# A top-32 attention with an MLP behind it: loads, MLP steps and the drain in another order

## The chip, the cores and the metric

One Trainium2 chip, one of its cores. The metric is the device time of one execution in microseconds (us), lower is better. Before the change three executions took 823.51, 825.10 and 825.77 us, median 825.10. An execution of the same kernel with the profiler on took 824.92 us.

## The reference

Inputs are q, k, v of shape (8 batches, 8 heads, 576 rows, 64), and an MLP with `w_in` (512 x 2048), `w_out` (2048 x 512) and `alpha` (2048). Per batch and head:

```
scores = (q @ k.T) / sqrt(64)                        # 576 x 576
kth    = the 32nd largest of each row
scores = where(scores >= kth, scores, -1e9)
attn   = exp(scores - max) / (sum + 1e-9)
o      = attn @ v                                    # 576 x 64
x      = o of all heads side by side                 # 4608 x 512
h      = x @ w_in                                    # 4608 x 2048
out    = (max(h, 0) + alpha * min(h, 0)) @ w_out     # 4608 x 512, float32
```

## The kernel before

**Duos.** The attention is cut into 144 duos of two 128 x 576 blocks of scores each, 18 a batch (lines 77 to 91; the drain's `D` is the last, 143). A pair p is two heads that share the 128 partitions. A normal duo `("n", p, j)` is rows 128j to 128j+127 of both heads; since 576 = 4 x 128 + 64, the last 64 rows of four pairs are packed into two "tails" duos `("m", ...)` a batch: duos 8, 9, 26, 27, 44, 45, 62, 63, 80, 81, 98, 99, 116, 117, 130 and 131. In the first six batches the order is j = 0 and 1, tails, j = 2 and 3.

**What a duo needs.** TensorE (PE) makes the scores in a PSUM tile of which there is one (`st_qk`, line 238; 6 matmul records for a normal duo, 16 for tails). ScalarE (ACT) copies them out (`st_exit`, 260). VectorE (DVE) finds a lower bound of the 32nd largest with MAX8 instructions (`dve_slot`, 317, and `threshold_steps`, 289); ACT counts what lies under it with Sign and an accumulator (`st_count`, 372); GpSimd (POOL) multiplies scores and signs (`st_y`, 384); DVE picks the exact value out of that (`row`, `pick_steps`). ACT then makes a large number of all that lies under the threshold with Relu, POOL subtracts it (`st_relu`, 391: two ACT and two POOL instructions), ACT takes Exp into the bf16 tile `w` (`st_exp`, 399), and a DMA transposes `w` into `wT` (`st_wT`, 404; three buffers). PE multiplies by v with a column of ones that gives the sum (`st_av`, 410), DVE divides (`norm_a`, `norm_b`) into the tile `x`, and a DMA transposes that into `xT` (`st_xT`, 467).

**The MLP.** Behind an `xT` stands a chunk of rows (`mlp_ready`, 494). A chunk has `unit`s (16 matmul records of 128 columns or 8 of 256 into one of two PSUM buffers `ph`, then one Relu into `gT`, `h_relu`, 564) and `part`s (five matmuls of 512 columns into `pz`, `o_pe`, 573), and at the end one ACT copy (`o_act`) and a store (`o_sp`). The prelu is folded into a second, linear weight, `w_lin`.

**The order.** It is written out by hand. The main loop (724 to 779) has a slot n for each duo, and within a slot each engine gets: on PE one `h_pe` or a filler (`keep_warm`, four matmuls on zeros), a transpose of q or k, the scores of duo n+1, `st_av` of an older duo, one `o_pe`, and at the end of the slot a second `o_pe` where enough is ready (765). `late` (742) adds one more `h_pe` in an even slot where many units wait. Loads of q, k and v are issued by SyncE (SP) in the middle of the slot (`run(n, "ld")`, 749), the two `xT` transposes of four pairs at its end (777 to 779). Every helper records its instructions in this order for its engine, and each engine, SP's DMA queue among them, works in it: an instruction that waits holds up all behind it.

**The drain.** What is left after slot 143 is a list of calls (808 to 890). There the last four duos but the first, 140 to 143, don't go through Relu and POOL: ACT takes Exp of all scores (`st_all`) and DVE masks them (`st_mask`, two instructions a duo). `T["spare"]` is the scores' PSUM, free by then. At the end `check_low` (678) looks whether any threshold came out invalid; if so a general path computes all again, which the drawn inputs don't need. The program ends when the last store has landed and the engines have met.

Of the kernel before, what the change touches and what calls it, by code (L numbers as in the profile page):

```python
# [12 lines left out]
ALU = mybir.AluOpType  # L13
# [46 lines left out]
def fast_path(tc, q, k, v, moe_w_in, moe_w_out, moe_alpha, out, flag):  # L60
# [32 lines left out]
    with ExitStack() as ctx:  # L93
# [171 lines left out]
        def norm_of(n):  # L265

            return stage.get(("norm", n), 0)

        def pick_steps(m):

            def eq_():
                sm(DVE.tensor_tensor(eq, io9.unsqueeze(1).to_broadcast([128, 4, 9]),
                                     T.pop(("cs", m)).unsqueeze(2).to_broadcast([128, 4, 9]), ALU.is_equal),
                   [(292, 301)], [(256, 292)])

            def pk_():
                pk = T["pk"] = two.tile([128, 4, 9], FP32, name="pk", tag="pk")
                sm(DVE.scalar_tensor_tensor(out=pk, in0=eq, scalar=BIG if m < ND // 2 - 2 else 1.0, in1=T.pop(("p9", m)), op0=ALU.mult,
                                            op1=ALU.mult), [(256, 292), f"p9{m % 3}"], ["pk"])
# [37 lines left out]
        def dve_slot(n, f_late):  # L317
# [19 lines left out]
            if n % 2:  # L337
                fold, negate, least, turn = threshold_steps(n // 2)
                fold()
                h_relu()  # L340
                negate()
            else:
                h_relu()
# [55 lines left out]
        def st_exp(n):  # L399
            w = ws[n % 4]  # L400
            ACT.activation(w[:, :, 0:S], T.pop(("s", n)), AF.Exp, scale=att_scale)
            st_wT(n)

        def st_wT(n):
# [89 lines left out]
        def mlp_ready(xt, rows):  # L494
# [229 lines left out]
        for n in range(ND):  # L724
# [26 lines left out]
            if ready() > 4 or not wide_copy:  # L751
                o_act()
# [36 lines left out]
        def st_mask(d):  # L789
            w, e, s_ = ws[d % 4], T.pop(("e", d)), T.pop(("s", d))  # L790
            for i in range(2):
                r = 2 * d + i
                DVE.scalar_tensor_tensor(out=w[:, i, 0:S], in0=s_[:, i, :], scalar=KT[:, r:r + 1],
                                         in1=e[:, i, :], op0=ALU.is_ge, op1=ALU.mult)
            st_wT(d)

        def normed(d):
            norm_a(d)
# [12 lines left out]
        o_sp()  # L811
        st_av(D - 6)
        h_pe(2)
        h_pe(2)
        h_relu(ACT)
        o_act()
        o_sp()
        st_count(D - 1)
        st_y(D - 1)
        h_relu()  # L820
        picked(D // 2 - 1)
        normed(D - 6)
        st_exp(D - 4)
        st_all(D - 3)
        row(D - 1, 0)
        row(D - 1, 1)
        st_count(D)
        st_y(D)
        st_all(D - 2)
        now[0] += 1  # L830
        fill(1)
        st_av(D - 5)
        fill(1)
        h_pe(2)
        fill(2)
        h_pe(2)
        st_av(D - 4)
        st_mask(D - 3)
        row(D, 0)
        row(D, 1)  # L840
        picked(D // 2)
        normed(D - 4)
        st_mask(D - 2)
        h_relu(ACT)
        st_all(D - 1)
        st_all(D)
        st_mask(D - 1)
        st_mask(D)
        o_act()
        o_sp()  # L850
        h_relu(ACT)
        h_pe(2)
        fill(1)
        st_av(D - 3)
        h_relu(ACT)
        h_pe(2)
        fill(1)
        st_av(D - 2)
        normed(D - 2)
        h_relu(ACT)  # L860
        o_act()
        o_sp()
        now[0] += 2
        h_pe(2)
        fill(1)
        st_av(D - 1)
        h_relu()
        h_pe(2)
        fill(1)
        st_av(D)  # L870
        normed(D)
        h_relu(ACT)
        o_act()
        o_sp()
        turn = 0
        while hq or act or soon or oq or stores:
            now[0] += 1
            while h_pe(2):
                pass
            o_pe()  # L880
            h_relu((DVE, ACT)[turn % 2])
            turn += 1
            if turn == 5:
# [288 lines left out]
```

## Time and profile before

| what | value |
|---|---|
| median of 3 executions | 825.10 us |
| profiled execution, its own time | 824.92 us |
| profiled execution, span of its instructions | 823.1 us |
| span of core 0, mean granted TensorE clock | 0.985 |
| first and last copy of scores out of PSUM | 9.42 and 769.94 us |
| last copy of a result out of PSUM starts | 815.22 us |

The span runs from the first to the last instruction; what lies around it is 1.8 us. Times in the rows are us from the span's start. In the rows of a time line the first number is the start, the second the time taken, and brackets at the end hold how long the engine sat idle before it and what ended that; "x4" behind a shape counts instructions that follow one another and were merged. PEld is TensorE's weight load. Every instruction of the fast path has line 32, the recording helper's, so rows are told apart by the tiles: `s_sb<-ps_sc` is the copy of scores, `sg` the Sign, `r` the Relu, `w` the Exp or the mask, `ph` a unit, `pz` or `spare<-w_out_b` a part, `rest` the filler, `tps` a transpose of q or k on PE, `xo` or `spare<-v,wT` is `st_av`.

### The profile page before, as it was taken

What the parts mean: (1) busy time and instruction counts of PE and PEld (TensorE: products, weight loads), DVE (VectorE), ACT (ScalarE), POOL (GpSimd) and SP (SyncE); (2) the same over time, 40 slices, a digit from 0 to 9 for tenths busy, and PEclk for the clock granted to TensorE, in tenths of its full rate; (3) what the DMA queues carried; (4) which work ended last, traced back from release to release, by engine and by line L of the source; (5) the groups of instructions that cost most, each with busy time, mean ns of one, the idle gap of its engine ahead of it and who ended that gap; (6) DMA issues with size and microseconds to landing.
All of it is one profiled execution on the core that took longest, in us unless ns stands there. A gap on an engine that the chain in (4) does not pass through costs nothing.

```text
span 823.1 us, 17793 instructions
## 1 busy us (share of the span) xinstructions
PE 734.9 (89%) x5351; PEld 424.2 (52%) x5426; DVE 757.5 (92%) x3471; ACT 763.3 (93%) x1257; POOL 745.5 (91%) x701
## 2 busy tenths in 40 slices
PE   8888899989999997988989898897989899999875
PEld 5334455555555554545555555454555555556553
DVE  4999999999999999998999999999899999999941
ACT  5999999999999999998999999999999999999921
POOL 2999999999998999999999999999999998999910
PEclk9999999999999999999999999999999999999989
DMA  7799996556564666665755556656566475544441
GB/s 157 174 192 189 155 170 115 104 119 120 127 134 105 120 126 131 116 123 106 133 109 118 118 113 134 122 128 113 110 130 136 97 122 107 97 98 87 83 85 50
DMA packets 343562, 100.25 MB, mean 122 GB/s; under 512 B 337425, under 2 KB 337441, under 8 KB 343457
## 3 DMA queue, kind: packets, MB, share of 16 engines
q1 hardware_dynamic: 340384, 91.90, 57.2%
q0 software_dynamic: 1872, 6.82, 3.6%
q8 instruction: 45, 0.74, 0.4%
q14 instruction: 61, 0.49, 0.2%
q10 hardware_dynamic: 1200, 0.30, 0.2%
HBM read 36.71 MB, written 9.44 MB: 56 GB/s over the span
## 4 chain that ended last, share of the span: by engine, by line
DVE 46%; PE 17%; ACT 17%; POOL 10%; issue 6%; DMA 3%; SPq 0%; DVEq 0%; ACTq 0%; POOLq 0%
DVE small L32 14%; DVE p L32 11%; DVE up L32 8%; DVE gT L32 5%; PE ps_sc L32 5%; POOL y L32 5%; POOL s_sb L32 5%; ACT r L32 5%; ACT sg L32 4%; PE pz L32 4%; ACT s_sb L32 4%; PE ph L32 4%; ACT w L32 2%; PE xo L32 2%; DVE qkT L32 2%
## 5 line engine op out<-in xcount | busy, mean ns | idle before, releaser
L32 POOL TENSOR_TENSOR y<-s_sb,sg 128x576 f32<-128x576 f32 x288 | 362.6, 1279 | 31.9 <-ACT sg L32 31.5
L32 POOL TENSOR_TENSOR s_sb<-s_sb,r 128x576 f32<-128x576 f32 x280 | 352.1, 1278 | 7.7 <-ACT r L32 7.1
L32 ACT ACTIVATE sg<-s_sb,p 128x576 bf16<-128x576 f32 x288 | 221.4, 773 | 8.3 <-DVE p L32 7.0
L32 DVE MAX8 p<-y 128x8 f32<-128x576 f32 x288 | 215.1, 747 | 6.2 <-POOL y L32 5.7
L32 DVE MAX8 up<-s_sb 128x8 f32<-128x96 f32 x864 | 211.9, 245 | 8.0 <-ACT s_sb L32 7.7
L32 DVE MAX8 small<-s_sb 128x8 f32<-128x96 f32 x864 | 216.0, 250 | 0.0
L32 ACT ACTIVATE r<-s_sb,KZ 128x576 bf16<-128x576 f32 x280 | 201.1, 769 | 0.3 <-DVE KZ L32 0.3
L32 PE MATMUL ps_sc<-qkT 64*128 64x512 f32 (+2 forms) x768 | 184.2, 570 | 16.9 <-ACT s_sb L32 16.7
L32 ACT COPY s_sb<-ps_sc 128x1152 f32<-128x1152 f32 x144 | 159.2, 1106 | 11.8 <-PE ps_sc L32 11.4
L32 ACT ACTIVATE w<-s_sb 128x1152 bf16<-128x1152 f32 x140 | 161.7, 1155 | 1.0 <-POOL s_sb L32 0.4
L32 PE MATMUL ph<-xT,w_in_b 128*128 128x256 bf16 (+1 forms) x1472 | 151.5, 251 | 11.2 <-DMA xT<-x 6.8
L32 PEld LDWEIGHTS <-w_in_b 128*128 128x128 bf16 x1472 | 120.6, 99 | 54.4 <-issue 10.8
L32 PE MATMUL pz<-w_out_b,gT 128*128 128x512 bf16 x513 | 133.9, 380 | 8.4 <-issue 6.7
L32 PE MATMUL xo<-v,wT 128*128 128x65 bf16 (+1 forms) x1560 | 123.5, 199 | 2.0 <-DVE x L32 1.5
L32 PEld LDWEIGHTS <-wT 128*128 128x128 bf16 (+3 forms) x1600 | 98.1, 100 | 36.6 <-DMA wT<-w 5.6
L32 DVE TENSOR_SCALAR gT<-ph 128x512 bf16<-128x512 f32 x136 | 91.7, 674 | 10.5 <-PE ph L32 10.5
L32 PEld LDWEIGHTS <-gT 128*128 128x128 bf16 x576 | 54.7, 98 | 69.4 <-issue 16.9
L32 PEld LDWEIGHTS ps_sc<-kd,qkT 128*128 128x128 f32 x256 | 38.5, 190 | 99.2 <-issue 97.4
L32 PEld LDWEIGHTS ps_sc<-qkT 64*128 64x128 f32 (+1 forms) x768 | 55.7, 170 | 60.0 <-issue 28.3
L32 PE MATMUL ps_sc<-kd,qkT 128*128 128x128 f32 x256 | 63.2, 329 | 1.0 <-DMA kd<-qkT 1.0
L32 PE MATMUL rest<-idle 128*128 128x512 bf16 x188 | 49.4, 390 | 7.5 <-DVE gT L32 5.4
L32 ACT ACTIVATION_READ_ACCUMULATOR sg<-s_sb,p 128x1 f32 x288 | 55.9, 194 | 0.0
(66 smaller groups left out, 582.7 us busy)
## 6 DMA issues: line engine op xcount, KB each, us to landing
k_st<-in_k_dram SPq DMA_DIRECT2D x64, 128.0 KB, 3.0
v_st<-in_v_dram SPq DMA_DIRECT2D x64, 128.0 KB, 2.9
q_st<-in_q_dram SPq DMA_DIRECT2D x62, 128.0 KB, 2.8
out_dram<-o_sb SPq DMA_DIRECT2D x31, 256.0 KB, 2.5
w_st<-in_moe_w_out_dram POOLq DMA_DIRECT2D x4, 1024.0 KB, 6.5
wT<-w SPq DMA_TRANSPOSE x144, 3.5
w_in_b<-in_moe_w_in_dram POOLq DMA_DIRECT2D x4, 512.0 KB, 6.2
k_st<-in_k_dram SPq DMA_DIRECT2D x32, 32.0 KB, 2.8
```

The costliest lines, as they stand in the source:

```text
L32: ins = self.tc.keep_in_program_order(f(*a, **kw))
```

## The change

Six edits:

1. In slots that end with a normalization, the loads are issued behind the two `xT` transposes instead of ahead of them.
2. The second `o_pe` of slot n is left out where duo n+2 is of the tails, and `late` is off where duo n+1 is: the parts and units come some slots later.
3. Duo 140 is masked like all before it, by Relu and POOL, and its `wT` is issued from ACT's DMA queue. Since pair 140/141 now has its thresholds multiplied by BIG, the mask of duo 141 multiplies them back (`kv`).
4. The order of the drain: among others `row` of duos 142 and 143 one behind the other; `wT` of 141 ahead of that of 140; `st_av` of 140 and 141 back to back, and of 142 and 143 apart from one unit; three parts in a row where there was one.
5. `unit`s in the drain need not wait two more steps of the counter `now`; the Relu of slot 143 goes to ACT.
6. `check_low` in the first turn of the last loop instead of the fifth.

The diff, with the lines that only move context left out:

```diff
-  scalar=BIG if m < ND // 2 - 2 else 1.0
+  scalar=BIG if m < ND // 2 - 1 else 1.0
...
                 fold()
-                h_relu()
+                if n < ND - 1:
+                    h_relu()
                 negate()
...
+        def st_wT(n, eng=SP):
             wt = three.tile([128, 10, 128], BF16, name="wT", tag="wT")
-            SP.dma_start_transpose(wt, w.rearrange("p a b -> p (a b)"))
+            eng.dma_start_transpose(wt, w.rearrange("p a b -> p (a b)"))
...
-                soon.append((now[0] + 2, lambda i=i: unit(i)))
+                soon.append((now[0] + 2 * (now[0] < ND), lambda i=i: unit(i)))
...
-            late = len(hq) > (9 if n < 118 else 4 if n < 132 else 3) and n % 2 == 0
+            late = len(hq) > (...) and n % 2 == 0 and not (on(n + 1) and duos[n + 1][0] == "m")
...
-            run(n, "ld")
+            if not norm_of(n):
+                run(n, "ld")
...
-            elif not ready() > (2 if n < 128 else 1) or not o_pe():
+            elif not ready() > (2 if n < 128 else 1) or on(n + 2) and duos[n + 2][0] == "m" or not o_pe():
                 if n and not did:
                     keep_warm()
...
             if norm_of(n):
                 st_xT(norm_of(n) - 1)
                 st_xT(norm_of(n))
+                run(n, "ld")
...
+            kt = KT[:, 2 * d:2 * d + 2]
+            if d == D - 2:
+                kt = two.tile([128, 2], FP32, name="kv", tag="kv", bufs=1)
+                DVE.tensor_scalar(kt, KT[:, 2 * d:2 * d + 2], 1.0 / BIG, None, ALU.mult)
```

The drain after the change, from the count of duo 142 on (the lines ahead of it gain one `h_relu(ACT)`):

```
        st_count(D - 1)
        st_y(D - 1)
        picked(D // 2 - 1)
        normed(D - 6)
        h_relu()
        st_exp(D - 4)
        st_count(D)
        st_y(D)
        for i in range(2):
            st_relu(D - 3, i)
        for d in (D - 1, D):
            row(d, 0)
            row(d, 1)
        st_all(D - 2)
        now[0] += 1
        o_pe()
        st_av(D - 5)
        o_pe()
        h_pe(2)
        o_pe()
        h_relu(ACT)
        h_pe(2)
        st_av(D - 4)
        picked(D // 2)
        normed(D - 4)
        h_relu(ACT)
        o_act()
        o_sp()
        h_pe(2)
        o_pe()
        st_all(D - 1)
        st_all(D)
        h_relu(ACT)
        st_mask(D - 2)
        st_exp(D - 3, ACT)
        o_pe()
        o_pe()
        o_act()
        o_sp()
        st_mask(D - 1)
        st_mask(D)
        for _ in range(2):
            h_pe(2)
            h_relu(ACT)
        st_av(D - 3)
        st_av(D - 2)
        normed(D - 2)
        h_pe(2)
        h_relu(ACT)
        st_av(D - 1)
        st_av(D)
        normed(D)
        h_pe(2)
        h_relu(ACT)
        now[0] += 2
        o_pe()
        o_pe()
        o_pe()
        o_act()
        o_sp()
        turn = 0
```

More of the change, by code (lines that the diff above doesn't have):

```diff
@@ L277, in pk_ @@
                 pk = T["pk"] = two.tile([128, 4, 9], FP32, name="pk", tag="pk")
-                sm(DVE.scalar_tensor_tensor(out=pk, in0=eq, scalar=BIG if m < ND // 2 - 2 else 1.0, in1=T.pop(("p9", m)), op0=ALU.mult,
+                sm(DVE.scalar_tensor_tensor(out=pk, in0=eq, scalar=BIG if m < ND // 2 - 1 else 1.0, in1=T.pop(("p9", m)), op0=ALU.mult,
                                             op1=ALU.mult), [(256, 292), f"p9{m % 3}"], ["pk"])
@@ L741, in fast_path @@
                 st_av(m)
-            late = len(hq) > (9 if n < 118 else 4 if n < 132 else 3) and n % 2 == 0
+            late = len(hq) > (9 if n < 118 else 4 if n < 132 else 3) and n % 2 == 0 and not (on(n + 1) and duos[n + 1][0] == "m")
             for m in duos_at("count", n):
@@ L813, in fast_path @@
         h_pe(2)
+        h_relu(ACT)
         h_pe(2)
@@ L819, in fast_path @@
         st_y(D - 1)
-        h_relu()
         picked(D // 2 - 1)
         normed(D - 6)
+        h_relu()
         st_exp(D - 4)
-        st_all(D - 3)
-        row(D - 1, 0)
-        row(D - 1, 1)
         st_count(D)
         st_y(D)
+        for i in range(2):
+            st_relu(D - 3, i)
+        for d in (D - 1, D):
+            row(d, 0)
+            row(d, 1)
         st_all(D - 2)
         now[0] += 1
-        fill(1)
+        o_pe()
         st_av(D - 5)
-        fill(1)
+        o_pe()
         h_pe(2)
-        fill(2)
+        o_pe()
+        h_relu(ACT)
         h_pe(2)
         st_av(D - 4)
-        st_mask(D - 3)
-        row(D, 0)
-        row(D, 1)
         picked(D // 2)
         normed(D - 4)
[L843 to L859, printed above, removed]
         h_relu(ACT)
@@ L862, in fast_path @@
         o_sp()
-        now[0] += 2
         h_pe(2)
-        fill(1)
+        o_pe()
+        st_all(D - 1)
+        st_all(D)
+        h_relu(ACT)
+        st_mask(D - 2)
+        st_exp(D - 3, ACT)
+        o_pe()
+        o_pe()
+        o_act()
+        o_sp()
+        st_mask(D - 1)
+        st_mask(D)
+        for _ in range(2):
+            h_pe(2)
+            h_relu(ACT)
+        st_av(D - 3)
+        st_av(D - 2)
+        normed(D - 2)
+        h_pe(2)
+        h_relu(ACT)
         st_av(D - 1)
-        h_relu()
-        h_pe(2)
-        fill(1)
         st_av(D)
         normed(D)
+        h_pe(2)
         h_relu(ACT)
+        now[0] += 2
+        o_pe()
+        o_pe()
+        o_pe()
         o_act()
@@ L882, in fast_path @@
             turn += 1
-            if turn == 5:
+            if turn == 1:
                 check_low()
```

12 lines of the change are left out of this document (5 added, 7 removed).

## The prediction

> **What bounds the kernel now.** First the page's busy times, then the loop cut into stretches of 18 duos (a batch), from one copy of scores to the one 18 duos later, and behind the last copy the drain.
>
> ```profile
> PE 734.9 (89%) x5351; PEld 424.2 (52%) x5426; DVE 757.5 (92%) x3471; ACT 763.3 (93%) x1257; POOL 745.5 (91%) x701
> ```
>
> ```profile
> 198.96:295.39 96.43, 88.39 (x659) 51.69 (x667) 93.89 (x434) 93.56 (x154) 93.05 (x85) 1.00 0.60 120
> 295.39:392.93 97.54, 86.60 (x606) 50.07 (x615) 92.88 (x433) 93.51 (x155) 95.19 (x87) 0.98 0.61 121
> 392.93:487.27 94.34, 85.38 (x644) 49.95 (x654) 92.24 (x431) 93.14 (x152) 90.47 (x83) 1.00 0.60 119
> 487.27:583.63 96.36, 84.34 (x601) 48.83 (x607) 92.80 (x433) 93.65 (x155) 95.33 (x87) 1.00 0.60 122
> 583.63:679.07 95.44, 86.01 (x650) 50.68 (x659) 92.91 (x432) 93.35 (x152) 91.71 (x86) 1.00 0.59 117
> 679.07:769.94 90.87, 86.82 (x717) 51.82 (x727) 88.60 (x409) 88.24 (x145) 86.64 (x75) 1.00 0.47 93
> ```
>
> The columns are the length, then PE, PEld, DVE, ACT and POOL busy, PE's clock, and DMA. ACT needs 93.1 to 93.7 us for every batch, whatever its length; what makes a batch long is ACT's idle time (96.43 - 93.56 = 2.9, 97.54 - 93.51 = 4.0, then 1.2, 2.7, 2.1 and 2.6 us, together 15.5). DVE (92.2 to 93.9 in the five full batches) and POOL (90.5 to 95.3) have hardly more room. So the loop is bound by three engines that are all nearly full, ACT first, and a change there can win at most those 15.5 us. Who ended ACT's waits over these six stretches:
>
> ```profile
> L32 ACT ACTIVATE sg<-s_sb,p 128x576 bf16<-128x576 f32 x214 | 164.5, 772 | 7.4 <-DVE p L32 6.4
> ...
> L32 ACT COPY s_sb<-ps_sc 128x1152 f32<-128x1152 f32 x108 | 119.2, 1104 | 7.7 <-PE ps_sc L32 7.3
> ```
>
> ```profile
> PE ph L32 <- DMA xT<-x: 6.8, 5, 2.2
> ```
>
> 7.3 us waited for PE's scores, although PE has 10% to spare: PE is late at single places. 6.4 us waited for DVE's threshold. PE itself waited 6.8 us for `xT`, five times.
>
> **Loads behind the transpose (edit 1).** The worst place, around duos 70 to 72:
>
> ```profile
> 373.96 1.96 SPq L32 DMA_DIRECT2D v_st<-in_v_dram  x3
> 374.50 0.40 DVE L32 TENSOR_TENSOR x<-xo,KZ 128x256 bf16<-128x256 f32 x1
> 375.96 1.79 SPq L32 DMA_DIRECT2D q_st<-in_q_dram  x3
> 377.86 2.54 SPq L32 DMA_TRANSPOSE xT<-x  x2
> 381.64 1.52 PE L32 MATMUL ph<-xT,w_in_b 128*128 128x256 bf16 x8 [2.13 <-DMA xT<-x]
> 386.32 1.12 ACT L32 COPY s_sb<-ps_sc 128x1152 f32<-128x1152 f32 x1 [1.94 <-PE ps_sc L32]
> 392.93 1.12 ACT L32 COPY s_sb<-ps_sc 128x1152 f32<-128x1152 f32 x1 [1.58 <-PE ps_sc L32]
> ...
> 583.63 1.12 ACT L32 COPY s_sb<-ps_sc 128x1152 f32<-128x1152 f32 x1 [1.58 <-PE ps_sc L32]
> ```
>
> ```profile
> 378.65:382.06 3.41, 1.28 (x8) 0.58 (x7) 3.38 (x19) 3.29 (x7) 3.41 (x4) 1.00 0.46 94
> 382.06:385.48 3.42, 3.42 (x14) 1.85 (x12) 2.05 (x7) 2.33 (x4) 3.36 (x4) 0.50 0.88 95
> ```
>
> `x` is written at 374.90, but SP issues six loads first and `xT` only from 377.86; PE reaches the unit that needs it at 379.5 and stands still 2.13 us. After that stretch with PE busy 1.28 of 3.41 us the clock is at 0.50 for the next 3.42, which costs another 1.7 us. With the loads behind, `xT` goes out at 374.9 to 377.5 and lands 2.9 us earlier (377.86 - 374.95), 0.8 us ahead of the need. So both copies' waits go, 1.94 + 1.58. The same step two batches later (duo 108) holds a wait for `xT` of up to 2.2 us without a drop of the clock, and ACT waits 1.58; that goes as well. What this edit moves: the loads start 3.5 us later at most. v is cast two slots on (10.6 us, a slot being 95.4 / 18 = 5.3), and the six issues take 1.96 + 1.79 us, so two slots of work cover them; without that cover POOL would wait up to those 3.5 us. `kd` and the next `wT`, queued behind on SP, go out 1 us later, and `wT` is used two slots on. These I cost at nothing.
>
> **MLP steps away from the tails (edit 2).**
>
> ```profile
> 249.10 1.03 PE L32 MATMUL pz<-w_out_b,gT 128*128 128x512 bf16 x4
> 249.96 1.06 PE L32 MATMUL ph<-xT,w_in_b 128*128 128x128 bf16 x16
> 253.03 1.12 ACT L32 COPY s_sb<-ps_sc 128x1152 f32<-128x1152 f32 x1 [1.41 <-PE ps_sc L32]
> ...
> 441.02 0.18 DVE L32 RECIPROCAL KZ<-xo 128x4 f32<-128x4 f32 x1 [1.17 <-PE xo L32]
> 447.56 0.78 ACT L32 ACTIVATE sg<-s_sb,p 128x576 bf16<-128x576 f32 x1 [0.70 <-DVE p L32]
> ...
> 638.27 0.78 ACT L32 ACTIVATE sg<-s_sb,p 128x576 bf16<-128x576 f32 x1 [0.69 <-DVE p L32]
> ```
>
> A part takes PE 1.08 us (its first matmul starts 0.22 ahead of the row at 249.10, and the next unit at 249.96), a unit 0.9. In the built order, PE has one part less ahead of the scores of duo 45 and one unit less ahead of 46: 2.0 us, against a wait of 1.41. Ahead of duos 80 and 81, and 116 and 117, there are two parts less each, 2.2 us against DVE's 1.17, which is what made the threshold late by 0.70 and 0.69. The same parts come back behind duos 47, 66, 67, 84, 102, 103, mostly in the place of fillers. A slot has 5.3 us; one with two parts, a unit, a transpose and scores has about 0.8 + 2.2 + 0.9 + 0.5 + 1.5 = 5.9 on PE, so two in a row put PE 1.2 us back, less than the 2 us by which its scores are normally early. I count a little for this below.
>
> Sum of the loop: 1.94 + 1.58 + 1.58 (edit 1) + 1.41 + 0.70 + 0.69 (edit 2) = 7.9 us; with all of the 7.3 us in place of the 6.5 quoted it is 8.7. DVE and POOL are near full too, and the returned parts cost something, so I take **7.5 us**; bounds 4 (half turns into waits for DVE and POOL) and 9.
>
> **The drain (edits 3 to 6).**
>
> ```profile
> wT<-w SPq DMA_TRANSPOSE x144, 3.5
> ```
>
> ```profile
> 780.19 2.56 DVE L32 SCALAR_TENSOR_TENSOR w<-s_sb,KZ,e_sb 128x576 bf16<-128x576 f32 x2
> ...
> 780.59 3.30 POOL L32 TENSOR_TENSOR y<-s_sb,sg 128x576 f32<-128x576 f32 x2 [1.10 <-ACT sg L32]
> ...
> 783.23 0.78 PE L32 MATMUL xo<-v,wT 128*128 128x65 bf16 x10
> ...
> 785.71 4.45 DVE L32 SCALAR_TENSOR_TENSOR w<-s_sb,KZ,e_sb 128x576 bf16<-128x576 f32 x6
> ...
> 799.27 0.60 ACT L32 ACTIVATE gT<-ph 128x512 bf16<-128x512 f32 x1 [12.91 <-PE ph L32]
> ...
> 800.15 0.78 PE L32 MATMUL spare<-v,wT 128*128 128x65 bf16 x10
> ...
> 804.81 1.07 PE L32 MATMUL ph<-xT,w_in_b 128*128 128x128 bf16 x16 [0.91 <-DMA xT<-x]
> ...
> 815.22 0.58 ACT L32 COPY o_sb<-spare 128x512 f32<-128x512 f32 x1 [2.79 <-PE spare L32]
> ```
>
> ```profile
> 787.32 4.69 DMA wT<-w
> ...
> 801.63 3.13 DMA xT<-x
> ```
>
> On DVE the two masks of duo 140 (2.56 us, beside POOL, against 4.45 / 6 = 0.74 each later) go, and a Relu of `ph`. ACT pays two Relus (0.77 each, as a Sign), POOL two subtractions (at most 1.65, as the products at 780.59) behind its last products, which end at 783.9; and behind ACT's waiting DMA stand one copy and two Relus of `ph`, for which PE's next units wait. All of this lies beside the chain: ACT then has 12.91 us of nothing to do. The first mask left, of duo 141, needs the normalization of 138/139, so PE's `st_av` at 783.23, which moves up about 0.4 with what DVE no longer does ahead of it; with 0.78 for that and 0.9 for reciprocal, product and `kv` the mask starts at about 784.5 instead of 785.71.
>
> From there the built program's waits make a new chain. ACT's transpose of 140 waits until that of 141, on SP, has landed; SP's transpose of 142 waits until that of 140 has landed; and 143 gets the buffer of 141, so it is issued only after `st_av(141)`. Before, the three went out behind one another. Masks of 141 end 786.0; `wT` lands with 4.7 at 790.7; the second, alone, with 3.5 at 794.2; `st_av` of 140 and 141, 1.6, at 795.8; the `wT` of 143 lands at 799.3; its `st_av` ends at 800.1 (before: 800.93, since it stood in PE's queue behind units; now the landings take that time). From there `x` +0.7, `xT` +3.1: 803.9 (before 804.8). PE fills that: one unit and three parts, 0.9 + 3.2, until 804.2. Behind it stand four units and five parts (3.6 + 5.4), where there were four and six, and the small matmul of `check_low`, which now waits up to 0.3 us for DVE: 9.4 against 10.4 us. At full clock the last copy starts at 813.6, 1.6 us earlier.
>
> But the clock:
>
> ```profile
> 788.25:791.66 3.41, 0.00 (x0) 0.00 (x0) 1.91 (x3) 0.00 (x0) 0.00 (x0) 1.00 1.06 168
> 791.66:795.07 3.41, 3.01 (x27) 2.52 (x28) 0.69 (x3) 0.00 (x0) 0.00 (x0) 0.50 0.75 158
> 795.07:798.49 3.42, 3.20 (x20) 1.91 (x20) 0.61 (x1) 0.00 (x0) 0.00 (x0) 0.50 0.00 0
> ```
>
> One empty stretch of 3.41 us, then two at half clock. The new order has PE idle from about 790.4 to 794.2 and again before 799.3, so I expect the same drop some 2 us later, reaching into the work behind 800, where each half-clock stretch costs 1.7 us. I take one such stretch at two thirds: **-0.5 us** for the drain, bounds -2 (no drop) and +3 (two stretches in the final part). The Trainium skill, "TensorE: Matmul & The Clock Gate", "What's actually happening", says that the clock falls after an idle window of about 3.4 us and returns after a busy one, on windows that run freely. The trace agrees with the length (3.41) but shows 3.01 of 3.41 busy not to be enough; by the page the drain would come out at -1.5.
>
> One store more goes through POOL's queue, the last stays on SP's; the scale of a threshold is a constant of the same instruction. Both nothing.
>
> Sum: 824.92 - 7.5 - 0.5 = 816.9; the profiled execution lies 0.2 under the median of the three, so 817.1.
>
> **The rivals.**
> (a) *Waits only change hands.* ACT, DVE and POOL are all within 3% of full, and PE gets the parts back at 47, 66 and 102. For it: DVE's waits for `up` and `p` stand behind nearly all ACT ones. Against: the stretch 392.93 to 487.27 already runs with ACT idle 1.2 us. Loop -4, drain -0.5: 820.6.
> (b) *The drain loses.* Serial landings of 4.7 instead of 3.5 and the clock down twice: drain +3, loop -7.5: 820.6, or +1 and 818.6. The Trainium skill, "DMA: Bandwidth & Descriptors", "Silent corruption: two transposing streams in flight at once", asks for just this wait between queues; no run here shows transposes of two queues at once. It speaks against edit 3: the second queue buys no overlap.
> (c) *The drain gains all.* No drop at all, loop in full (-9): 824.9 - 9 - 2 = 814.
> (d) *Slower than before.* The clock stays at half from about 792 to the end because each 3.41 us stretch holds a wait (for `wT`, `xT`, the evacuations): the 13.5 us of PE work behind 800 take up to twice that, +13.5 - 1.6. Five half-clock stretches (8.5) eat the loop's gain; it decides from there on. Price: 824.9 - 7.5 + 10 = 827.4. Against: before, the clock was back at 798.5.
>
> **How the numbers follow.** Forecast 0.57 (815 to 819), (a) 0.14, (b) 0.13, (c) 0.10, (d) 0.06. The range reaches over (a) and (b) and just below the forecast, 814 to 822. A measurement of this kernel tells about 0.3%, 2.5 us, from no change. Faster by more (under 822.6): the forecast, (c) and most of (a) and (b), 0.86; within 0.3%: 0.07; slower: (d) and what I don't see, 0.07.
>
> **What would show it.** PE's waits for `xT` in the loop gone (6.8 us over five), ACT's wait for `ps_sc` behind 199 us from 7.3 to under 2, the stretch with duos 54 to 71 from 97.5 to about 94; last copy of scores at 762 to 763. In the drain `wT` of 140 issued when that of 141 lands, the last `st_av` 30 us behind the last copy of scores (before 30.2), clock 0.50 somewhere behind it. It is wrong if the batches keep their length though the waits for `ps_sc` are gone, or if the drain from the last copy of scores (53.1 us) changes by over 3.

## The result, and the profile after

The changed kernel takes 817.46 us (median of 4 executions, 817.19 to 818.90) against 825.43 us for the kernel before, measured beside it: a ratio of 0.9912, 95% interval 0.9892 to 0.9931, so faster by 6 to 9 us. (The ratio comes from all executions; the quotient of the two medians is 0.9903.) Forecast were 817.1 us and a range of 814 to 822. The profiled execution took 817.19 us, its span is 815.3. Of all executions in this document one, of the kernel with edits 3 to 6 below, took 988.54 us at a granted clock of 0.654, and the ratio of that kernel leaves it out.

First the busy times of the page, then the same six stretches of 18 duos, cut again from one copy of scores to the one 18 duos later. The columns are those of before.

```profile
PE 743.0 (91%) x5438; PEld 424.2 (52%) x5438; DVE 754.3 (93%) x3467; ACT 765.9 (94%) x1262; POOL 747.6 (92%) x704
```

```profile
198.93:294.40 95.47, 88.81 (x666) 51.64 (x664) 94.12 (x435) 93.54 (x154) 93.91 (x86) 1.00 0.61 121
294.40:388.31 93.91, 88.56 (x632) 50.53 (x630) 92.69 (x433) 93.47 (x153) 92.31 (x85) 1.00 0.63 122
388.31:482.03 93.72, 86.53 (x648) 49.65 (x649) 92.26 (x430) 93.22 (x153) 92.72 (x84) 1.00 0.61 123
482.03:577.17 95.14, 86.58 (x614) 49.14 (x611) 92.85 (x433) 93.69 (x154) 94.18 (x86) 1.00 0.61 124
577.17:671.43 94.26, 87.22 (x661) 50.62 (x659) 92.92 (x432) 93.16 (x153) 92.45 (x87) 1.00 0.57 119
671.43:762.30 90.87, 87.91 (x727) 51.81 (x727) 88.76 (x409) 88.35 (x144) 86.82 (x75) 1.00 0.46 93
```

ACT's work per stretch is what it was, 93.2 to 93.7 us. Its idle time fell from 15.5 us to 7.9 (the sum of the lengths, 563.37, less that of its busy times, 555.43), and the last copy of scores moved from 769.94 to 762.30. The stretch with duos 54 to 71 gained most, 97.54 to 93.91. The same groups and the same wait as before, in the loop of the changed kernel (the last line from the list of all waits):

```profile
L32 ACT ACTIVATE sg<-s_sb,p 128x576 bf16<-128x576 f32 x214 | 164.4, 771 | 5.3 <-DVE p L32 4.4
...
L32 ACT COPY s_sb<-ps_sc 128x1152 f32<-128x1152 f32 x107 | 117.9, 1102 | 1.8 <-PE ps_sc L32 1.8
```

```profile
PE ph L32 <- DMA xT<-x: 1.3, 1, 1.3
```

ACT's wait for scores went from 7.3 to 1.8 us, its wait for the threshold from 6.4 to 4.4, PE's for `xT` from 6.8 to 1.3. The place around duos 70 to 72, in order of time:

```profile
373.57 0.41 DVE L32 TENSOR_TENSOR x<-xo,KZ 128x256 bf16<-128x256 f32 x1
374.01 2.50 SPq L32 DMA_TRANSPOSE xT<-x  x2
376.60 1.79 SPq L32 DMA_DIRECT2D v_st<-in_v_dram  x3
378.25 1.04 PE L32 MATMUL ph<-xT,w_in_b 128*128 128x256 bf16 x8
...
383.40 1.10 ACT L32 COPY s_sb<-ps_sc 128x1152 f32<-128x1152 f32 x1
```

`xT` goes out 0.03 us behind `x`, and neither the unit nor the copy has a bracket any more: nothing waits. The 1.8 us that are left of ACT's wait for scores are two new places:

```profile
294.40 1.12 ACT L32 COPY s_sb<-ps_sc 128x1152 f32<-128x1152 f32 x1 [0.78 <-PE ps_sc L32]
...
567.51 1.05 PE L32 MATMUL ph<-xT,w_in_b 128*128 128x256 bf16 x8 [1.34 <-DMA xT<-x]
572.06 0.18 DVE L32 RECIPROCAL KZ<-xo 128x4 f32<-128x4 f32 x1 [1.19 <-PE xo L32]
577.17 1.12 ACT L32 COPY s_sb<-ps_sc 128x1152 f32<-128x1152 f32 x1 [0.99 <-PE ps_sc L32]
```

They are duos 54 and 108. Ahead of duo 54 the built order now has a late unit that was not there, and PE then waits 1.07 us for DVE's Relu behind it. The wait at duo 108 starts at the unit of the second row. PE reaches that unit at 566.17 us, 4.4 behind the end of `x` (561.75), as it does with edit 1 alone (4.5). But the second transpose of `x` took 4.5 us to land, where 2.5 is the rule (in the list of DMA from 564 to 566 us the last number is the time from issue to landing):

```profile
q8 instruction: 1, 0.02, 3.0%
...
xT<-x SPq DMA_TRANSPOSE x1, 4.5
```

PE's wait of 1.34 us for it is handed on: DVE waits 1.19 for `st_av`, and ACT 0.99 for the scores. In the five kernels here with this loop (see the table below) ACT's wait at duo 108 is 0.58 to 0.99 us and PE's for `xT` 0.93 to 1.34, each time 0.35 more. In these five the transpose took 4.1 to 4.5 us, and a packet of the instruction queue (q8 in the list, 16 KB, about 1 us long) lies inside that time; in the six others with edit 1 it landed in 2.5, and the packet came behind it. Whether the packet is the cause no run tests.

The drain, from the last copy of scores to the last copy of a result, took 815.22 - 769.94 = 45.28 us and now takes 807.39 - 762.30 = 45.09. Its chain, as the changed kernel's time line has it, and the clock beside it:

```profile
776.85 1.55 DVE L32 SCALAR_TENSOR_TENSOR w<-s_sb,kv,e_sb 128x576 bf16<-128x576 f32 x2
...
784.09 1.47 ACTq L32 DMA_TRANSPOSE wT<-w  x1
...
787.65 2.07 PE L32 MATMUL spare<-v,wT 128*128 128x65 bf16 x20 [5.98 <-DMA wT<-w]
789.64 1.89 PE L32 MATMUL ph<-xT,w_in_b 128*128 128x128 bf16 x16
...
792.68 0.79 PE L32 MATMUL spare<-v,wT 128*128 128x65 bf16 x10 [0.43 <-DMA wT<-w]
...
807.39 0.59 ACT L32 COPY o_sb<-spare 128x512 f32<-128x512 f32 x1 [2.68 <-PE spare L32]
```

```profile
781.40:784.81 3.41, 0.27 (x5) 0.09 (x2) 0.00 (x0) 0.00 (x0) 0.00 (x0) 1.00 0.11 24
784.81:788.23 3.42, 0.58 (x7) 0.43 (x8) 0.00 (x0) 1.57 (x3) 0.56 (x1) 0.50 0.68 162
788.23:791.64 3.41, 3.41 (x35) 2.88 (x35) 0.61 (x2) 0.07 (x1) 0.00 (x0) 0.50 0.93 180
791.64:795.05 3.41, 2.98 (x39) 2.20 (x37) 0.61 (x2) 1.07 (x2) 0.00 (x0) 1.00 0.13 23
```

PE stands idle for 6 us until `wT` of 140 has landed, then works at half clock until 791.64, then waits 0.43 us for `wT` of 143; behind that it works with hardly a gap. Nearly the whole gain, 7.6 of 7.8 us in the spans, is the loop's.

### The profile page after: what moved, and what is told of

Same layout as the page of the kernel before. It is cut to its first block, busy times and chain, and to the rows that moved or that the text cites. A ratio compares the mean times of both kernels' runs of the same rounds, so it can differ in the third digit from the quotient of the medians.

```text
span 815.3 us, 17917 instructions
## 1 busy us (share of the span) xinstructions
PE 743.0 (91%) x5438; PEld 424.2 (52%) x5438; DVE 754.3 (93%) x3467; ACT 765.9 (94%) x1262; POOL 747.6 (92%) x704
## 4 chain that ended last, share of the span: by engine, by line
DVE 41%; PE 18%; ACT 17%; POOL 14%; issue 7%; DMA 2%; SPq 0%; ACTq 0%; POOLq 0%; DVEq 0%
DVE small L32 13%; DVE p L32 10%; DVE up L32 8%; POOL y L32 7%; POOL s_sb L32 6%; DVE gT L32 5%; PE ps_sc L32 5%; ACT r L32 4%; PE pz L32 4%; ACT sg L32 4%; PE ph L32 4%; ACT s_sb L32 4%; ACT w L32 3%; PE xo L32 2%; DVE qkT L32 1%
## 5 line engine op out<-in xcount | busy, mean ns | idle before, releaser
L32 PE MATMUL pz<-w_out_b,gT 128*128 128x512 bf16 x544 | 139.8, 379 | 0.0
L32 DVE TENSOR_SCALAR gT<-ph 128x512 bf16<-128x512 f32 x133 | 89.8, 675 | 6.8 <-PE ph L32 6.8
L32 PE MATMUL pz<-w_lin_b,xT 128*128 128x512 bf16 (+1 forms) x152 | 52.8, 389 | 11.1 <-ACT o_sb L32 10.6
L32 PE MATMUL rest<-idle 128*128 128x512 bf16 x200 | 53.3, 394 | 8.5 <-DVE gT L32 6.4
```

Source lines behind the costliest of these rows:

```text
L32: ins = self.tc.keep_in_program_order(f(*a, **kw))
```

## The experiments

The theory: the loop makes the gain, edit 1 about two thirds of it and edit 2 a third; the drain is worth nothing, because its second queue makes the landings serial. Rivals: the two loop edits stand in for one another; the drain has a merit of its own that something hides. All times of the runs, each against the kernel before on its own chip; "loop" is from the first to the last copy of scores and "drain" from there to the start of the last copy of a result, both in the profiled execution. The medians of the kernel before were 825.43 us beside the changed kernel, 824.96 beside the four runs behind it, 823.63 beside the next four, 824.62 beside the three after these and 824.55 beside the last, so between these groups the ratios compare, not the times:

| run | us | ratio, 95% interval | loop | drain |
|---|---|---|---|---|
| before | 825.43 | 1 | 760.5 | 45.28 |
| after | 817.46 | 0.9912, 0.9892 to 0.9931 | 753.0 | 45.09 |
| edit 1 alone | 819.24 | 0.9936, 0.9919 to 0.9953 | 754.6 | 44.99 |
| edit 2 alone | 825.53 | 1.0006, 0.9990 to 1.0022 | 760.5 | 43.65 |
| edits 1 and 2 | 817.23 | 0.9903, 0.9885 to 0.9921 | 753.0 | 45.28 |
| edits 3 to 6 | 825.91 | 1.0016, 1.0006 to 1.0026 | 760.6 | 45.90 |
| after, one queue | 816.80 | 0.9908, 0.9893 to 0.9922 | 752.5 | 45.07 |
| after, one queue, tile of its own | 815.71 | 0.9897, 0.9882 to 0.9911 | 753.1 | 44.33 |
| after, fillers | 818.40 | 0.9930, 0.9917 to 0.9943 | 752.8 | 46.37 |
| after, parts in even batches | 816.61 | 0.9907, 0.9891 to 0.9922 | 751.5 | 46.00 |
| after, one queue, own tile, even batches | 814.70 | 0.9874, 0.9851 to 0.9897 | 751.5 | 44.83 |
| the same and fillers (the combined kernel) | 811.30 | 0.9840, 0.9821 to 0.9858 | 751.4 | 41.05 |
| that, and no late unit in slot 52 | 812.68 | 0.9861, 0.9837 to 0.9884 | 751.7 | 41.50 |
| edits 1, 2 in even batches, old drain, fillers | 815.18 | 0.9891, 0.9874 to 0.9908 | 751.6 | 43.78 |

**Edit 1 alone** (the kernel before with the loads behind `xT`):

```diff
-            run(n, "ld")
+            if not norm_of(n):
+                run(n, "ld")
...
                 st_xT(norm_of(n))
+                run(n, "ld")
```

> Edit 1 alone: the loads behind the two transposes of x, all else as before. Theory of the prediction: ACT's waits of 1.94 and 1.58 us (duos 71, 72) and that of duo 108 go; in the changed kernel the stretch 295.39 to 392.93 was 3.6 us shorter, and one half of the 1.58 of duo 108 came back as a wait of 0.99, so the whole is 4.2 to 5.1 us faster (819.9 to 821.2 where before is 825.0), the stretch with duos 54 to 71 at about 94, and PE's waits for xT gone. Rival, the two loop edits stand in for one another (the parts that edit 2 takes from PE are what makes the transposes of x come in time): under 2.5 us faster, and a wait for xT stays.

5.7 us faster by the medians, a little more than the theory. Two stretches of its trace, those with duos 54 to 71 and 90 to 107:

```profile
295.49:389.31 93.82, 85.24 (x614) 49.74 (x624) 92.87 (x434) 93.35 (x154) 93.21 (x86) 1.00 0.60 126
...
483.78:577.61 93.83, 84.22 (x604) 49.04 (x611) 92.82 (x434) 93.40 (x154) 93.41 (x86) 1.00 0.60 123
```

Both now run with ACT idle for 0.5 us or less: 97.54 - 93.82 = 3.7 and 96.36 - 93.83 = 2.5 us. The others kept their lengths within 0.2. So edit 1 is worth more than the theory allowed for the second place (2.5 against 1.58), since nothing comes back at duo 108 here.

**Edit 2 alone:**

```diff
-            late = ... and n % 2 == 0
+            late = ... and n % 2 == 0 and not (on(n + 1) and duos[n + 1][0] == "m")
...
-            elif not ready() > (2 if n < 128 else 1) or not o_pe():
+            elif not ready() > (2 if n < 128 else 1) or on(n + 2) and duos[n + 2][0] == "m" or not o_pe():
```

> Edit 2 alone: no second part ahead of the tails and no late unit there. Theory of the prediction: ACT's waits at duos 46, 82 and 118 go (1.41, 0.70, 0.69), 2.4 to 2.8 us faster (822.2 to 822.6 where before is 825.0); the stretch with duos 54 to 71 keeps its 97.5 us. Rival, the parts that come back behind duos 66 and 67 meet the wait for xT at duo 70: that stretch grows by 1 to 2 us and the edit alone is worth 1 us or nothing.

No gain that shows: the rival holds in the number and in the kind of wait, but not in the place. The stretches with duos 54 to 71 and 90 to 107:

```profile
294.72:392.60 97.88, 88.80 (x617) 50.71 (x625) 92.78 (x432) 93.68 (x153) 94.43 (x86) 0.98 0.60 120
...
486.28:585.07 98.79, 86.62 (x605) 49.89 (x611) 93.05 (x433) 93.85 (x154) 95.27 (x87) 0.98 0.59 119
```

```profile
574.11 1.89 PE L32 MATMUL ph<-xT,w_in_b 128*128 128x256 bf16 x8 [3.01 <-DMA xT<-x]
...
578.47 1.12 ACT L32 COPY s_sb<-ps_sc 128x1152 f32<-128x1152 f32 x1 [2.29 <-PE ps_sc L32]
```

The first, which the rival named, grew by 0.3 us, the second by 2.4, which eats what the other stretches win (0.96, 0.66 and 1.23). PE's wait for `xT` there is 3.0 us now where it was 2.15, the clock falls behind it (0.98 in the mean, 1.89 us where a unit takes 1.04), and ACT waits 2.29. PE does not come to it earlier than before: it reaches the unit 4.4 us behind the end of `x` here and 4.5 before. The second transpose took 3.5 us to land in place of 2.5. The twelve executions lie between 821.53 and 828.17 us, the longer ones with a lower mean clock (0.977 at 828.17, 0.988 at 822.01), so how much edit 2 alone is worth differs with where the clock falls.

**Edits 1 and 2, old drain** (both diffs above):

> Edits 1 and 2 with the old drain. Theory: the loop makes the whole gain, last copy of scores at 762 to 763 and the drain 53 us as before, so the time is that of the changed kernel within 0.5 us (7.2 to 7.9 us faster than before). Rival, the new drain needed what the new loop left over and the old drain is slower behind it: last copy of scores at 762 to 763, but only 5 to 6.5 us faster.

The theory holds: 817.23 us, loop and drain as in the changed kernel.

**Edits 3 to 6, old loop** (the changed kernel without the two diffs above):

> Edits 3 to 6 with the old loop. Theory from the two traces: drain 53.0 against 53.1 us, the time within 0.5 us of before. The prediction had 0.5 us faster for this part. Rival, the drain does gain 1.5 to 2 us with its own merits, and lost them in the changed kernel because the new loop hands it more units and parts: 823.0 to 823.5 where before is 825.0.

1 us slower (ratio 1.0016, 1.0006 to 1.0026); the drain took 45.90 us, the loop what it takes before. (The profiled execution's first copy of scores is at 11.16 us, 1.7 later than before, ahead of all that these edits touch; loop and drain are free of that.) Neither the half microsecond that was forecast nor the rival's 1.5 to 2 is there.

**One queue in the drain:**

```diff
-        st_exp(D - 3, ACT)
+        st_exp(D - 3)
```

> The changed kernel with the transpose of duo 140 in SP's queue behind that of 141, not in ACT's. Theory: the two queues make each transpose wait for the landing of the one before; in one queue the landings lie 1.1 to 1.4 us apart as before the change. wT of 140 then lands at about 785.0 (787.60 in the changed kernel), that of 142 at 786.3 (791.19), that of 143 still waits for its buffer and lands 790.2 (792.63). The first idle time of PE shrinks from 6.0 to 3.4 us, the second grows by up to 1.7: 1.0 to 2.4 us faster than the changed kernel (815.1 to 816.5 where that is 817.5). Rival, the order of the work and the buffer set the end and the queue costs nothing: within 0.5 us of the changed kernel.

The transposes did come earlier, and against the changed kernel it bought nothing. In its time line the `st_av` of 140 and 141 starts 23.67 us behind the last copy of scores, 25.35 in the changed kernel, and the work behind runs at half clock until 795 (a unit of 16 records 1.89 us, a part 1.73):

```profile
785.60 2.07 PE L32 MATMUL spare<-v,wT 128*128 128x65 bf16 x20 [4.28 <-DMA wT<-w]
...
791.30 1.89 PE L32 MATMUL ph<-xT,w_in_b 128*128 128x128 bf16 x16
```

The number is the rival's, but not its reason.

**And a tile of its own for duo 143:**

```diff
-            wt = three.tile([128, 10, 128], BF16, name="wT", tag="wT")
+            if n < ND - 1:
+                wt = three.tile([128, 10, 128], BF16, name="wT", tag="wT")
+            else:
+                wt = stg.tile([128, 10, 128], BF16, name="wT", tag="q_st", bufs=2)
```

> As the run before, and the transpose of duo 143 goes into a tile of its own (in a staging tile of q, free by then), so that it waits for no st_av. Theory: all four landings follow at 1.1 to 1.4 us, the last at about 788, PE has 3.4 us of idle time left and the last st_av ends at 789.5 (793.47 in the changed kernel): 2.5 to 3.5 us faster than the changed kernel (814.0 to 815.0). Rival, x's transpose and the units behind it become the bound: last st_av early, but PE waits for xT and the end moves by less than 1.5 us.

The drain is 0.8 us shorter, against 2.5 to 3.5 by the theory, and PE does not wait for `xT`, so the rival's reason falls too, though its number (under 1.5) holds. The picture is that of the run before: from 785.8 to about 794 PE works without a gap and at half clock.

**Fillers ahead of the late `st_av`:**

```diff
+        ps = ps_x.tile([128, 2, 2, 65], FP32, name="rest", tag="x")
+        for i in range(40):
+            PE.matmul(ps.rearrange("p a b c -> p (a b c)")[:, 0:256], idle, idle.unsqueeze(1).to_broadcast([128, 2, 128]), start=(i == 0), stop=(i == 39))
         st_av(D - 3)
```

> The changed kernel with 40 matmuls of 256 columns on zeros (about 4.3 us) in PE's idle time ahead of the st_av of duo 140; they serve no result. It asks what the half clock of the drain costs. Theory: the clock stays at 1.00, the 20 matmul records of the two st_av take 1.56 in place of 2.07 us, so wT of 143 goes out 0.5 us earlier and the end comes 0.5 us earlier; the other slow matmuls lie beside the landings. Rival 1, the two slow stretches cost their 1.7 us each as the prediction took for one of them at two thirds: 1.1 to 3.4 us faster. Rival 2, the clock falls in spite of the fillers: no change.

Rival 2 comes nearest. The drain is 46.37 us, 1.3 longer than in the changed kernel but only 0.4 to 0.5 longer than in two other kernels with that drain (45.90 and 46.00), and the intervals of the two ratios overlap. From its time line and its stretches:

```profile
786.91 1.52 PE L32 MATMUL spare<-v,wT 128*128 128x65 bf16 x20 [1.19 <-DMA wT<-w]
...
790.49 0.79 PE L32 MATMUL spare<-v,wT 128*128 128x65 bf16 x10 [1.05 <-DMA wT<-w]
...
792.63 1.73 PE L32 MATMUL ph<-xT,w_in_b 128*128 128x128 bf16 x16
```

```profile
789.42:792.84 3.42, 1.74 (x25) 1.29 (x25) 0.11 (x1) 0.60 (x1) 0.00 (x0) 1.00 0.61 115
792.84:796.25 3.41, 3.19 (x20) 2.07 (x19) 0.50 (x2) 0.60 (x1) 0.00 (x0) 0.50 0.24 43
```

The fillers did keep the clock over the first idle time (1.52 us for the two `st_av`, not 2.07), but PE then waits three times for serial landings, 1.19, 1.05 and 0.63 us, and the clock falls at 792.8, where the work no longer lies beside a landing.

**The second part left out in even batches only** (ahead of duos 44, 80 and 116; in the changed kernel):

```diff
-            ... or on(n + 2) and duos[n + 2][0] == "m" or not o_pe():
+            ... or on(n + 2) and duos[n + 2][0] == "m" and n // 18 % 2 == 0 or not o_pe():
```

> The changed kernel, but the second part is left out ahead of the tails of duos 44, 80 and 116 alone, not ahead of 62, 98 and 130. Theory: ahead of 62 and 98 PE had room, and what comes back at 102 and 103 makes DVE wait 1.18 and ACT 0.99 us at duo 108; with edit 1 alone that stretch took 93.83 us and with both 95.15. So the stretch from duo 90 to 108 comes to 93.8 to 94.0 and the kernel is 1.1 to 1.4 us faster than the changed one. Rival, the wait at duo 108 comes from elsewhere (the phase of PE against ACT, handed on from the batch before): no change, or the wait turns up some duos on.

The theory's number holds: the stretch with duos 90 to 107 is back at its length with edit 1 alone, and the loop is 1.4 us shorter:

```profile
482.14:575.93 93.79, 84.62 (x604) 49.20 (x614) 92.84 (x434) 93.34 (x155) 93.18 (x86) 1.00 0.59 122
```

Its reason is not in the trace. PE reaches the unit ahead of duo 108 no earlier than in the changed kernel (4.5 us behind the end of `x`); what is gone is the late landing of `xT`, 2.5 us in place of 4.5.

In the time itself it doesn't stand out (0.9907 against 0.9912), since the drain of the profiled execution took 0.9 us more. The drain of edits 3 to 6 ran the same instructions in 45.09, 45.90 and 46.00 us in three kernels. In the first it has two stretches at half clock, in the others three; the last two of this kernel, at the clock's own edges:

```profile
788.64:792.06 3.42, 3.10 (x33) 2.41 (x32) 0.61 (x2) 0.60 (x1) 0.00 (x0) 0.50 0.22 41
792.06:795.47 3.41, 3.19 (x13) 1.59 (x13) 0.00 (x0) 0.60 (x1) 0.00 (x0) 0.50 0.19 38
```

**All of it together, without and with fillers.** The first joins three of the edits above (even batches, one queue, the tile of its own), the second puts 30 matmuls of 256 columns ahead of `st_av(D - 3)`, as above.

> The loop rule of the run for 62, 98 and 130 together with the drain of one queue and a tile of its own for duo 143, no fillers. Theory: both add up, the loop's last copy of scores 1.0 to 1.2 us earlier than in the changed kernel and the drain from it 0.7 to 0.8 shorter; 9.2 to 10 us faster than before (815.0 to 815.8 where before is 825.0). In the drain all of PE's work from the first late st_av on stands in one row, with two to three stretches at half clock in it. Rival: the earlier loop only makes the drain wait longer for the store and the transposes, under 8.5 us faster.

> The same with 30 matmuls of 256 columns on zeros (3.4 us) in PE's idle time of 3.6 us ahead of the st_av of duo 140. Theory: what the earlier landings won was lost to the clock, since PE's work behind them, 785.8 to 794.9, ran at half speed (20 matmul records 2.06 and 2.09 for 1.52 us, two units 1.89 for 1.06, one part 1.48 for 1.03). With PE kept busy the clock stays at 1.00 and those 3.2 us go: 2.5 to 3.2 us faster than the run without fillers; PE then waits for the last xT at most a few tenths. Rival 1: the clock falls later all the same, as with the 40 fillers ahead of late landings, and the gain is under 0.5 us. Rival 2: xT and the copies behind ACT take its place, 1 to 2 us.

814.70 us, 9.9 faster than before, and 811.30. The first sum is right with its parts off: against the changed kernel the loop is 1.5 us shorter (1.0 to 1.2 in the theory), the drain 0.3 (0.7 to 0.8). From the time lines of the two kernels, first without fillers, then with:

```profile
783.67 2.01 PE L32 MATMUL spare<-v,wT 128*128 128x65 bf16 x20 [3.54 <-DMA wT<-w]
...
805.59 0.59 ACT L32 COPY o_sb<-spare 128x512 f32<-128x512 f32 x1 [2.68 <-PE spare L32]
```

```profile
780.29 3.44 PE L32 MATMUL rest<-idle 128*128 128x256 bf16 x30
784.33 1.51 PE L32 MATMUL spare<-v,wT 128*128 128x65 bf16 x20 [0.60 <-DMA wT<-w]
...
802.11 0.59 ACT L32 COPY o_sb<-spare 128x512 f32<-128x512 f32 x1 [2.69 <-PE spare L32]
```

And their clock over that time, cut at its own edges:

```profile
780.37:783.78 3.41, 0.10 (x4) 0.11 (x4) 0.00 (x0) 0.40 (x1) 0.00 (x0) 1.00 1.24 215
783.78:787.19 3.41, 3.41 (x35) 2.77 (x35) 0.60 (x2) 0.00 (x0) 0.00 (x0) 0.50 0.65 128
787.19:790.61 3.42, 3.42 (x36) 2.78 (x35) 0.60 (x2) 0.60 (x1) 0.00 (x0) 0.50 0.00 0
790.61:794.02 3.41, 3.19 (x13) 1.49 (x13) 0.00 (x0) 0.60 (x1) 0.00 (x0) 0.50 0.19 38
```

```profile
781.84:785.25 3.41, 2.81 (x32) 2.17 (x29) 0.00 (x0) 0.00 (x0) 0.00 (x0) 1.00 1.09 275
785.25:788.67 3.42, 3.42 (x56) 2.89 (x53) 1.02 (x4) 0.60 (x1) 0.00 (x0) 1.00 0.27 51
```

The theory holds, a little above its 2.5 to 3.2: 30 matmuls that compute nothing save 3.4 us of time (no execution with them is over 812.06, none without them under 813.01) and 3.8 us of drain. This version beats both kernels: 0.9840 (0.9821 to 0.9858) against the changed kernel's 0.9912 (0.9892 to 0.9931).

**No late unit in slot 52:**

```diff
-            late = ... and not (on(n + 1) and duos[n + 1][0] == "m")
+            late = ... and not (on(n + 1) and duos[n + 1][0] == "m") and n != 52
```

> As the run before, and no late unit in slot 52 (edit 2 pushed one there; ACT waits 0.78 us for the scores of duo 54). Theory: that wait goes and nothing takes its place: 0.6 to 0.8 us faster than the run before, the stretch with duos 36 to 53 at 94.7 instead of 95.5. Rival: the unit and the parts that move to 57, 61, 66 and 83 make another wait: no change or slower by up to 1 us.

The rival. Duos 36 to 53 win what the theory said (0.9 us), and duos 72 to 89 give it back, with 94.99 us where the changed kernel has 93.72 and the combined one 93.73, and more of ACT's own work in it:

```profile
386.89:481.88 94.99, 88.26 (x661) 51.41 (x669) 93.27 (x433) 93.94 (x155) 92.98 (x85) 1.00 0.63 121
```

**The old drain with fillers** (the kernel before with edit 1, edit 2 in even batches, and 27 such matmuls ahead of `st_av(D - 3)`):

> The loop of the run for 62, 98 and 130, with the drain of before (all four wT in SP's queue, duo 140 masked by DVE) and 27 matmuls of 256 columns on zeros (3.0 us) ahead of the st_av of duo 140, where PE stands idle for 3.0 us. It asks whether the new order of the drain is worth something of its own once the clock is kept. From the last copy of scores to the last copy of a result the old drain took 45.28 us without fillers, the new one with one queue, a tile of its own and fillers 41.05. Theory: the old order wins only the 1.0 to 1.7 us of its own slow stretches and then waits for the last xT, since its masks stand 1.8 us apart: 43.5 to 44.3 us, the kernel at 813.5 to 814.5 where before is 825.0. Rival: the order is worth nothing and the clock was all: 41 to 42 us, 811 to 812.

A drain of 43.78 us, as the theory said; the median, 815.18, lies 0.7 above its range, the profiled execution (814.42) inside. From 773.31 us to the end of PE's work the clock stays at 1.00, but one stretch of the drain ahead of that ran at half clock:

```profile
769.90:773.31 3.41, 3.41 (x18) 1.86 (x18) 3.03 (x3) 3.19 (x6) 2.30 (x3) 0.50 0.81 101
```

So of the 43.78 - 41.05 = 2.7 us between the old drain and that of the combined kernel up to 1.7, half of this stretch, may be the clock's. What is left is the worth of the new order together with one queue and the tile of its own, not of the order alone. And the old drain without fillers took 43.65 to 45.28 us in four kernels, so a gain by fillers isn't shown for it.

## Why the prediction was right, and where it was not

**The bound** (ACT, by its idle time): right. ACT's work per stretch did not change, and the loop got shorter by what left its idle time: 15.5 - 7.9 = 7.6 us. The signs named for it came: the last copy of scores at 762.30, ACT's wait for scores at 1.8 us, the stretch with duos 54 to 71 at 93.91.

**Edit 1** was put at 5.1 us (1.94 + 1.58 + 1.58) and is 5.9 of loop alone (760.5 - 754.6). The mechanism is as told: `xT` goes out at once, PE's wait and the slow stretch behind it are gone. Mis-sized was the second place, 1.58 for 2.5. Which of the two places has the drop of the clock isn't fixed: the kernel with edits 3 to 6 runs the loop of before, with the same waits of PE for `xT`, and there the clock falls at the second place, where ACT then waits 1.57 us in place of 0.21 (duo 107), and not at the first, where it waits 0.28 in place of 1.94 (duo 71). Edit 1 takes away both. The loads that go out later cost nothing that can be seen.

**Edit 2** was put at 2.8 us (1.41 + 0.70 + 0.69). Behind edit 1 it is 754.6 - 753.0 = 1.6, in even batches only 754.6 - 751.5 = 3.1, alone nothing that shows. The waits that it named did go: against edit 1 alone the stretches with duos 36 to 53, 72 to 89 and 108 to 125 are 0.96, 0.75 and 1.27 us shorter. Too small was the price of what comes back, 0.4 us in the sum: the stretch with duos 90 to 107 is 1.31 longer, and the 0.96 already holds a new wait of 0.78 at duo 54. The step that failed is "so two in a row put PE 1.2 us back, less than the 2 us by which its scores are normally early": it adds up PE's own work and holds no wait. At duo 54 PE waits 1.07 us for DVE's Relu behind the late unit that the fuller list brings into slot 52. At duo 108 it is not put back by the parts of 102 and 103 at all; it waits 1.34 us for an `xT` that landed late. The run with even batches takes the second away; the first moved elsewhere when it was taken away. And the terms of the two edits were added up as if each stood by itself: without edit 1, edit 2 met a wait for `xT` of 3.0 us in place of 2.15.

**The loop's sum**, 7.5, came out at 7.6 because one term was 0.8 too small and the other 1.2 too large, and 0.4 had been taken off for what the returned parts cost. That it came so close is luck in part.

**The drain** was put at -0.5 with bounds -2 and +3, and is -0.2 in the two profiles; edits 3 to 6 alone make the kernel 0.5 to 2.1 us slower. The mask of 141 starts 776.85 - 762.30 = 14.55 us behind the last copy of scores, where 784.5 - 769.94 = 14.56 was forecast, and the waits are those named: ACT's queue, then SP's, then the buffer. Two terms were off in the changed kernel, and they nearly cancel, by luck. `wT` of 141 took 5.4 us to land (4.7 in the sum), `wT` of 140 is in use 25.35 us behind (forecast 24.3), and the two `st_av` took 2.07 us (1.52 with fillers), so the last `st_av` ends 31.2 behind (forecast 30.2). And **the clock** step, "the same drop some 2 us later, reaching into the work behind 800", 30 us behind the last copy of scores, did not come there: the empty stretch began 19.1 us behind (781.40 - 762.30), 0.8 later than before (788.25 - 769.94 = 18.3), PE was nearly idle in the first slow one too (0.58 of 3.42 us), and the second ended 29.3 behind. The work behind the last `st_av` then took 13.9 us.

In the two other kernels with this drain (edits 3 to 6; parts in even batches) the steps came as told. `wT` of 141 landed in 3.4 and 3.8 us, the last `st_av` ended 29.8 and 29.9 us behind the last copy of scores, three slow stretches ended 34.2 and 34.4 behind, and the work behind the last `st_av` took 16.1 us. So the drop costs 16.1 - 13.9 = 2.2 us there, for which the sum had 1.1, and the drain is 0.6 to 0.7 us longer than before, not 0.5 shorter.

By the Trainium skill, "TensorE: Matmul & The Clock Gate", "What's actually happening", the clock falls after an idle window of about 3.4 us and returns after a busy one. The traces agree on the length, but the busy time of the profile doesn't settle what counts as idle or busy. At the clock's own edges stretches with PE busy 0.00, 0.10, 0.27, 1.28, 1.74 and 1.87 of 3.41 us were followed by half clock and one with 2.08 by full clock, but so was one with 1.79 (one queue, 805.07 to 808.49). At half clock 3.41 us of work brought the full clock back in the changed kernel, while in the combined kernel without its fillers two stretches with 3.41 and 3.42 did not, and the third, with 3.19, did. The same page says that the windows run freely; that fits the same drain having two slow stretches in one kernel and three in two others.

**The rivals.** (a), waits that change hands, is true of 1.8 us, not of half. (b) was right in its reason, that the second queue buys no overlap (the Trainium skill, "DMA: Bandwidth & Descriptors", "Silent corruption: two transposing streams in flight at once", wants exactly that wait, and here it moves the landing of 140 by 1.7 us); against the changed kernel its price was zero, since the clock took what one queue alone would have given, and against the two kernels that have three slow stretches as well it was 0.8 to 0.9 us (45.90 and 46.00 to 45.07). (c) asked for a drain without a drop of the clock and put it at -2; with fillers, one queue and the tile, which is more than it spoke of, it is -4.2 (45.28 - 41.05). (d) did not happen.

What stays open: why the second transpose of `x` lands in 4.1 to 4.5 us ahead of duo 108 with edits 1 and 2, and in 3.5 with edit 2 alone, where it takes 2.5 elsewhere. In the first case a packet of the instruction queue lies inside the landing time; but in the drain, where one lies inside the time of `wT` of 141 in the three kernels with edits 3 to 6, that landing took 3.4, 3.8 and 5.4 us. No run moves that packet alone.

## What to carry to other kernels

Where several engines are nearly full, add up the idle times of the one that bounds and look at which wait ends last at each; but work that is only moved turns up at another such place, so look for the next tight point behind where it lands, and look there at what each engine waits for before you blame the work that was moved. Two edits that touch the same wait aren't additive: run each alone and both. In a drain, look at the clock ahead of the last chain: an earlier transfer is worth little if the work behind it then runs at half clock, and fillers helped here when they reached to the moment from which PE had work without gaps. A single profile of such a stage can be off by about 1 us: compare several kernels that share it.

## What the runs showed of the hardware

- Fillers do not always help: 40 of them kept the clock over 4.5 us, and it fell 8 us later, in the work behind the last `st_av` (drain 46.37 us, without them 45.09 to 46.00 in three kernels); 30 ahead of gapless work won 3.8.
- What a stretch of 3.41 us at half clock costs, by the loop of before in two kernels: ACT waits 1.94 us with it and 0.28 without it at duo 71, 1.57 and 0.21 at duo 107, so 1.7 and 1.4 us.
- At half clock a stretch with PE busy 3.41 of 3.41 us brought full clock back once (788.23 to 791.64 in the changed kernel); in the combined kernel without its fillers two such stretches did not, and the third did.
- In the drain a transpose of `w` that waited for the landing of the one before took 3.5 us to land (784.09 to 787.60 in the changed kernel), one that follows another in SP's queue 5.3 in the combined kernel with fillers. Two in one queue are still ready sooner than two of which the second waits for the first to land: the `st_av` that needs them starts 23.67 us behind the last copy of scores with one queue, 25.35 in the changed kernel.
